# The last query tile of each batch takes the 64 rows that are left, in a fused attention and two-layer feed-forward kernel

## The chip, the cores and the metric

The kernel runs on one core of a Trainium2 chip. The metric is the device time of one execution in microseconds. The profile is of one execution; the runs that are compared are others.

## What is computed

The reference, cut to what matters (B = 8 batches, H = 8 heads, S = 576 rows, D = 64; all in float32):

```python
k_p = k.reshape(B, H, 72, 8, D).mean(axis=3)
v_p = v.reshape(B, H, 72, 8, D).mean(axis=3)
scores = scale * np.matmul(q, k_p.transpose(0, 1, 3, 2))
scores = scores - np.max(scores, axis=-1, keepdims=True)
attn = np.exp(scores)
attn = attn / (np.sum(attn, axis=-1, keepdims=True) + 1e-09)
attn_out = np.matmul(attn, v_p)

x = attn_out.transpose(0, 2, 1, 3).reshape(4608, 512)
h = x @ w_in
x = np.maximum(0.01 * h, h) @ w_out

rms = np.sqrt(np.mean(x * x, axis=-1, keepdims=True) + 1e-06)
xn = x / rms * rms_g
g = xn @ w_gate
out = (g * (1.0 / (1.0 + np.exp(-g))) * (xn @ w_val)) @ w_out2
```

## The kernel before

The program has three parts: attention, a first feed-forward layer (512 to 2048 to 512) and a second one (512 to 1536 to 512, with normalisation and gate). Attention is woven into the first layer: while the matmuls of one tile of 512 tokens of that layer run, the attention steps of later tokens are put between them. That weave fills the first 880 us; the second layer follows.

Attention goes batch by batch, 40 query tiles in all. The 576 query rows of a batch are five tiles of 128 (list `QT`, line 52), the fifth of which starts at row 448, so that its first 64 rows are rows of the fourth, taken again. The steps of a query tile (b, t) are:

- `load_q` (line 217): one DMA on SP's queue, 128 rows by 8 heads by 64 numbers, in pieces of 256 bytes.
- `step_t` (line 299): four TensorE transposes against the identity `ident`, tile `qt` (line 303), and a copy of the result to `qT` on ScalarE (line 308).
- `step_s` (line 313): four matmuls with the pooled keys, tiles `sc` (line 325), with `qT` as the stationary operand and 144 columns moving. The softmax runs with the query rows on the partitions: maximum, subtraction, exponential, sum, reciprocal, product (lines 331 to 340).
- `step_x` (line 347): the small copies `er` (line 363), four transposes `xt` (line 369), two transposes `xr` from 96 columns (line 374). From the result ScalarE writes the high halves of the weights, `at` (`split`, line 92) and `atr` (line 376), and VectorE their low halves (lines 95 and 378). Of the fifth tile the first 64 columns were left out here (`skip`).
- `step_av` (line 390): once both or all three tiles of a chunk (256 or 320 rows) are there, for each pair of heads three matmuls with `at` (line 395) and one with `atr` (line 400), tile `av`; its result is split into the tokens `xhl` of the first layer.

The names in the profile carry batch, chunk or tile: `at1_0` holds the weights of batch 1 (counted from 0), chunk 0; `xt1_1` the transposes of batch 1, tile 1; `xt2_4` those of the fifth tile of batch 2. In the profile's rows these numbers are left out.

Beside this, the first layer's weights come in during the first 130 us (`class Weights`): `load` (line 130, a DMA from SP), `begin` (a ScalarE and a VectorE instruction on the raw tile, lines 138 and 141), `end` (lines 149, 92 and 95). The last of them are loaded in halves, such as `raw_o14_256` and `raw_i15_256`, into three slots that they share with the loads of keys and values. In the first layer `h` (line 592) is x @ w_in for 512 tokens and 128 hidden columns, `ghl` its activation, `y` (line 628) the product with w_out; `y_store` (line 635) copies a finished `y` tile to `ye`, on ScalarE or VectorE by turns, and stores it.

The code gives each engine its instructions in program order, but for the first 880 us the framework's scheduler may put them in another order on each engine, by its own estimates of durations. That order is fixed when the program is built; on the chip each engine works through its list, and an instruction that waits holds up those behind it on the same engine.

Of the kernel before, what the change touches and what calls it, by code (L numbers as in the profile page):

```python
# [8 lines left out]
F32 = mybir.dt.float32  # L9
# [4 lines left out]
ALU = mybir.AluOpType  # L14
# [8 lines left out]
def pooled_attention_then_two_ffns(  # L23
# [13 lines left out]
    nc = tc.nc  # L37
    B, H, S, D = q.shape
    NT, DM = out.shape
    P = 128  # L40
    POOL = 8
    SP = S // POOL
    NP = H // 2
# [5 lines left out]
    W = 2 * P  # L49
    N = 512  # L50
    NJ = NT // N
    QT = [0, 128, 256, 384, S - P]
    RB = [0, 128, 256, 384, H * SP - P]
    CH = [(0, 256, (0, 1)), (256, S, (2, 3, 4))]
    CHMAX = 320
# [4 lines left out]
    REST = 2 * SP - P  # L60
    R1 = 2 * REST
    R3 = 3 * R1
# [6 lines left out]
    def bank(tag, bufs, name):  # L69
        return ps.tile([P, 512], F32, tag=tag, bufs=bufs, name=name)  # L70
# [7 lines left out]
    def scratch(b, name, early=False):  # L78

        return bank("att", 2, name) if b else bank("ya" if early else "yb", 2, name)  # L80

    ident = per.tile([P, P], F32, name="ident")
# [6 lines left out]
    def split(hi_eng, hi, lo_eng, lo, src):  # L89

        if hi_eng is nc.scalar:
            nc.scalar.activation(out=hi, in_=src, func=AF.Copy)  # L92
        else:
            hi_eng.tensor_copy(out=hi, in_=src)
        lo_eng.tensor_tensor(out=lo, in0=src, in1=hi.bitcast(F32), op=ALU.subtract)  # L95
# [8 lines left out]
    def rows(w, f):  # L104
        return w[f * P:(f + 1) * P, :]
# [62 lines left out]
    att = tc.tile_pool(name="att", bufs=1)  # L168
    ap = att.__enter__()
# [5 lines left out]
    for h, sign in ((0, -1), (1, 1)):  # L175
        nc.gpsimd.affine_select(
            out=mask_main[:, h:h + 1], in_=mask_main[:, h:h + 1], compare_op=ALU.is_ge, fill=0.0,
# [4 lines left out]
    for sign, base in ((1, 0), (-1, REST - 1)):  # L182
        nc.gpsimd.affine_select(
            out=group, in_=group, compare_op=ALU.is_ge, fill=0.0, base=base, channel_multiplier=sign,
# [4 lines left out]
        out=mask_rest[:, :, 1], in_=group.rearrange("p d q -> p q d"), axis=AX.X, op=ALU.add  # L189
# [27 lines left out]
    def load_q(b, t, tile_=None):  # L217
        x = ap.tile([P, 512], F32, tag="q", bufs=2, name=f"q{b}_{t}") if tile_ is None else tile_
        nc.sync.dma_start(
            out=x.rearrange("p (h d) -> p h d", h=H),  # L220
            in_=q[b, :, QT[t]:QT[t] + P, :].rearrange("h s d -> s h d"),
        )
        qraw[b, t] = x

# [74 lines left out]
    def step_t(b, t):  # L299
        pt = scratch(b, f"qt{b}_{t}", early=t < 2)  # L300
        x = qraw.pop((b, t))
        for c in range(NP):
            nc.tensor.transpose(pt[:, c * P:(c + 1) * P], x[:, c * P:(c + 1) * P], ident)  # L303
        if b == 0 and t % 3:
            y = per.tile([P, NP, P], F32, tag=f"w{23 + t % 3}", bufs=1, name=f"qT{b}_{t}")
        else:
            y = ap.tile([P, NP, P], F32, tag="qT", bufs=1, name=f"qT{b}_{t}")
        nc.scalar.copy(out=y.rearrange("p c n -> p (c n)"), in_=pt)
        qT[b, t] = y

    ex = {}
# [1 line left out]
    def step_s(b, t):  # L313
        y = qT.pop((b, t))
        if b == 0:
            e = per.tile([P, H, SP], F32, tag=f"w{20 + t % 4}", bufs=1, name=f"ex{b}_{t}")
        else:
            e = ap.tile([P, H, SP], F32, tag="ex", bufs=1, name=f"ex{b}_{t}")
        st = ap.tile([P, 3, H], F32, tag="st", bufs=2, name=f"st{b}_{t}")
        n = 2 * SP  # L320
        for half in range(2):
            pt = bank("att", 2, f"sc{b}_{t}_{half}")
            for i in range(2):
                p = 2 * half + i
                nc.tensor.matmul(  # L325
                    pt[:, i * n:(i + 1) * n], y[:, p, :], kblk[b % 2][:, p * n:(p + 1) * n],
                    start=True, stop=True,
                )
            s = pt[:, 0:2 * n].rearrange("p (h c) -> p h c", h=4)
            hs = slice(4 * half, 4 * half + 4)  # L330
            nc.vector.tensor_reduce(out=st[:, 0, hs], in_=s, axis=AX.X, op=ALU.max)
            nc.vector.tensor_tensor(
                out=e[:, hs, :], in0=s, in1=st[:, 0, hs].unsqueeze(2).to_broadcast([P, 4, SP]),
                op=ALU.subtract,
            )
        nc.scalar.activation(out=e, in_=e, func=AF.Exp, scale=ESCALE)
        nc.vector.tensor_reduce(out=st[:, 1, :], in_=e, axis=AX.X, op=ALU.add)
        nc.vector.tensor_scalar(out=st[:, 1, :], in0=st[:, 1, :], scalar1=1e-9, scalar2=None, op0=ALU.add)
        nc.vector.reciprocal(out=st[:, 2, :], in_=st[:, 1, :])
        nc.vector.tensor_tensor(  # L340
            out=e, in0=e, in1=st[:, 2, :].unsqueeze(2).to_broadcast([P, H, SP]), op=ALU.mult
        )
        ex[b, t] = e

# [2 lines left out]
    def step_x(b, t):  # L347
        ci = 0 if t < 2 else 1
        c0 = CH[ci][0]
        if (b, ci) not in at:  # L350
            at[b, ci] = (
                ap.tile([P, NP, 2, CHMAX], F32R, tag="at", bufs=1, name=f"at{b}_{ci}"),
                ap.tile([R3, 2, CHMAX], F32R, tag="atr", bufs=1, name=f"atr{b}_{ci}"),
            )
        a, ar = at[b, ci]
        e = ex.pop((b, t)).rearrange("p (c h) k -> p c (h k)", h=2)
        new = QT[t] if t < 4 else QT[3] + P
        skip = new - QT[t]
        n = P - skip
        cols = slice(new - c0, new - c0 + n)  # L360
        er = ap.tile([P, 2, 3, R1], F32, tag="er", bufs=1, name=f"er{b}_{t}")
        for g in range(2):
            (nc.scalar.copy if b < 2 else nc.vector.tensor_copy)(
                out=er[:, g].rearrange("p d (q k) -> p d q k", q=2),
                in_=e[:, 2 * g:2 * g + 2, P:].unsqueeze(1).to_broadcast([P, 3, 2, REST]),
            )
        pt = scratch(b, f"xt{b}_{t}")
        for c in range(NP):
            nc.tensor.transpose(pt[:, c * P:(c + 1) * P], e[:, c, 0:P], ident)  # L369
        src = pt.rearrange("p (c n) -> p c n", n=P)[:, :, skip:]  # L370
        split(nc.scalar, a[:, :, HI, cols], nc.vector, a[:, :, LO, cols], src)
        pt = scratch(b, f"xr{b}_{t}")
        for g in range(2):
            nc.tensor.transpose(pt[0:R3, g * P:(g + 1) * P], er[:, g].rearrange("p d k -> p (d k)"), ident)
        src = pt[0:R3, 0:2 * P].rearrange("p (g n) -> p g n", n=P)[:, :, skip:]
        nc.scalar.activation(out=ar[:, :, cols], in_=src, func=AF.Copy)
        z = slice(R1, 2 * R1)
        nc.vector.tensor_tensor(
            out=ar[z, :, cols], in0=src[z], in1=ar[z, :, cols].bitcast(F32), op=ALU.subtract
        )  # L380
# [171 lines left out]
    for n in range(2 * F1):  # L552
        key = ("io"[n % 2], n // 2)
        src = rows(w_out, n // 2) if n % 2 else cols(w_in, n // 2)
# [13 lines left out]
    for i in range(0, len(first), 2):  # L568
# [3 lines left out]
        t = per.tile([P, 2, 512], F32, tag=f"w{24 + i // 2}", bufs=1, name=f"first{i}")  # L572
# [689 lines left out]
```

## Time and profile before

| | us |
| --- | --- |
| median of 3 runs | 1808.96 (1805.79 to 1812.09) |
| the profiled execution | 1812.26 |
| its span | 1810.5 |
| PE busy (matmul) | 1758.0 (97%) |
| DVE, ACT, POOL busy | 891.1 (49%), 670.4 (37%), 551.2 (30%) |

PE is TensorE's matmuls, PEld its weight loads, DVE is VectorE, ACT ScalarE, POOL GpSimd and SP the engine that issues the DMAs. The span is the profiled execution from its first instruction to its last; its time is the 1810.5 us and 1.8 us around it. Matmuls are pipelined: the duration of a record is longer than the distance from one to the next, so costs on PE are read from the starts of groups. A number in square brackets at the end of a timeline row is the time that the engine stood idle before it, with the instruction or DMA that ended this.

### The profile page before, as it was taken

What the parts mean: (1) busy time and instruction counts of PE and PEld (TensorE: products, weight loads), DVE (VectorE), ACT (ScalarE), POOL (GpSimd) and SP (SyncE); (2) the same over time, 40 slices, a digit from 0 to 9 for tenths busy, and PEclk for the clock granted to TensorE, in tenths of its full rate; (3) what the DMA queues carried; (4) which work ended last, traced back from release to release, by engine and by line L of the source; (5) the groups of instructions that cost most, each with busy time, mean ns of one, the idle gap of its engine ahead of it and who ended that gap; (6) DMA issues with size and microseconds to landing.
All of it is one profiled execution on the core that took longest, in us unless ns stands there. A gap on an engine that the chain in (4) does not pass through costs nothing.

```text
span 1810.5 us, 23634 instructions
## 1 busy us (share of the span) xinstructions
PE 1758.0 (97%) x8596; PEld 1498.0 (83%) x8596; DVE 891.1 (49%) x1603; ACT 670.4 (37%) x1424; POOL 551.2 (30%) x681
## 2 busy tenths in 40 slices
PE   3899999999999999999999999999999999999999
PEld 2889887878888888888888888899788889978887
DVE  7974435454356555455344345345534444553331
ACT  5754333443344444344343332243232323322220
POOL 2653303334125142211110442154144204413320
PEclk6999999999999999999999999999999999999999
DMA  8833204447365555435451766687775668776562
GB/s 253 307 109 89 55 21 143 157 140 230 101 189 157 163 157 162 145 125 180 157 172 45 234 195 211 228 300 245 255 245 196 193 226 314 245 250 224 186 209 93
DMA packets 175555, 330.81 MB, mean 183 GB/s; under 512 B 54352, under 2 KB 90192, under 8 KB 174928
## 3 DMA queue, kind: packets, MB, share of 16 engines
q1 hardware_dynamic: 175440, 329.31, 56.1%
q8 instruction: 68, 1.11, 0.3%
q14 instruction: 47, 0.39, 0.1%
HBM read 277.87 MB, written 51.38 MB: 182 GB/s over the span
## 4 chain that ended last, share of the span: by engine, by line
PE 89%; DVE 5%; DMA 3%; issue 1%; ACT 1%; SPq 1%; POOL 1%; ACTq 0%; DVEq 0%; POOLq 0%
PE y L628 20%; PE h L592 20%; PE o L1089 16%; PE yg L1014 6%; PE yv L1014 6%; PE xv L1014 4%; PE xg L1014 4%; PE wg L1014 4%; PE wv L1014 4%; PE sc L325 2%; PE av L395 1%; PE xt L369 1%; DMA wo<-wo 1%; PE qt L303 1%; DMA y<-ye 1%
## 5 line engine op out<-in xcount | busy, mean ns | idle before, releaser
L592 PE MATMUL h<-xhl,w_i 128*128 128x512 f32 (+1 forms) x1824 | 438.2, 385 | 3.1 <-ACT xhl L92 1.3
L592 PEld LDWEIGHTS h<-xhl,w_i 128*128 128x128 f32 x1824 | 329.5, 191 | 68.3 <-DVE xhl L95 4.1
L1089 PE MATMUL o<-wo,u 128*128 128x512 f32 x1296 | 315.1, 390 | 3.5 <-DMA wo<-wo 3.4
L628 PE MATMUL y<-ghl,w_o 128*128 128x512 f32 (+1 forms) x1296 | 285.1, 365 | 1.4 <-DVE ghl L605 1.4
L1089 PEld LDWEIGHTS o<-wo,u 128*128 128x128 f32 x1296 | 242.0, 188 | 53.0 <-DMA wo<-wo 4.9
L628 PEld LDWEIGHTS y<-ghl,w_o 128*128 128x128 f32 x1296 | 218.9, 191 | 35.1 <-DVE ghl L605 1.8
L605 DVE TENSOR_TENSOR ghl<-g,ghl 128x512 fp32r<-128x512 f32 (+1 forms) x152 | 114.6, 754 | 241.5 <-ACT g L98 238.3
L98 ACT ACTIVATE ghl<-h 128x512 fp32r<-128x512 f32 (+1 forms) x152 | 87.0, 572 | 233.4 <-PE h L592 232.9
L628 PE MATMUL y<-ghl,wr 128*128 128x512 f32 x624 | 158.9, 395 | 0.0
L628 PEld LDWEIGHTS y<-ghl,wr 128*128 128x128 f32 x624 | 115.1, 188 | 22.4
L95 POOL TENSOR_TENSOR u<-e2g,u 128x512 fp32r<-128x512 f32 (+1 forms) x25 | 29.7, 1190 | 308.3 <-ACT u L92 308.3
L229 POOL TENSOR_TENSOR v<-v 128x256 f32<-128x256 f32 (+2 forms) x84 | 59.7, 713 | 107.6 <-DMA v<-in_v_dram 105.0
L98 ACT ACTIVATE g<-h 128x512 f32<-128x512 f32 (+1 forms) x152 | 86.8, 571 | 1.0 <-DVE ghl L605 1.0
L1014 PE MATMUL yg<-T,ag 128*128 128x512 f32 (+1 forms) x360 | 84.0, 368 | 0.0
L1014 PE MATMUL yv<-T,av 128*128 128x512 f32 (+1 forms) x360 | 83.8, 368 | 0.0
L1014 PE MATMUL xg<-xa,ag 128*128 128x512 f32 (+1 forms) x360 | 83.8, 367 | 0.0
L1014 PE MATMUL xv<-xa,av 128*128 128x512 f32 (+1 forms) x360 | 83.7, 367 | 0.0
L1014 PEld LDWEIGHTS yg<-T,ag 128*128 128x128 f32 x360 | 66.0, 188 | 10.0 <-DVE e1v L991 0.6
L1014 PEld LDWEIGHTS yv<-T,av 128*128 128x128 f32 x360 | 66.2, 188 | 9.5
L1014 PEld LDWEIGHTS xv<-xa,av 128*128 128x128 f32 x360 | 66.0, 188 | 9.6
L1014 PEld LDWEIGHTS xg<-xa,ag 128*128 128x128 f32 x360 | 66.1, 188 | 9.4
L735 POOL TENSOR_TENSOR parts_g<-raw_g,parts_g 128x256 fp32r<-128x256 f32 (+1 forms) x48 | 33.7, 727 | 102.7 <-ACT parts_g L731 102.7
(166 smaller groups left out, 2596.2 us busy)
## 6 DMA issues: line engine op xcount, KB each, us to landing
wo<-wo SPq DMA_DIRECT2D x120, 512.0 KB
av<-op_v SPq DMA_DIRECT2D x90, 512.0 KB
ag<-op_g SPq DMA_DIRECT2D x90, 512.0 KB
wr<-wo SPq DMA_DIRECT2D x52, 512.0 KB
y<-ye SPq DMA_DIRECT2D x36, 256.0 KB
op_g<-parts_g SPq DMA_DIRECT2D x36, 256.0 KB
op_v<-parts_v SPq DMA_DIRECT2D x36, 256.0 KB
out_dram<-oe SPq DMA_DIRECT2D x36, 256.0 KB
```

What stands on the lines that cost most here:

```text
L95: lo_eng.tensor_tensor(out=lo, in0=src, in1=hi.bitcast(F32), op=ALU.subtract)
L98: return nc.scalar.activation(out=out, in_=in_, func=AF.Prelu, scale=scale, alpha=alpha)
L229: nc.gpsimd.tensor_tensor(out=x[:, :n], in0=x[:, :n], in1=x[:, n:2 * n], op=ALU.add)
L303: nc.tensor.transpose(pt[:, c * P:(c + 1) * P], x[:, c * P:(c + 1) * P], ident)
L325: nc.tensor.matmul(pt[:, i * n:(i + 1) * n], y[:, p, :], kblk[b % 2][:, p * n:(p + 1) * n], start=True, stop=True,)
L369: nc.tensor.transpose(pt[:, c * P:(c + 1) * P], e[:, c, 0:P], ident)
L592: nc.tensor.matmul(pt, w[:, sp, c * P:(c + 1) * P], x[:, mp, c, :], start=c == 0 and i == 0, stop=c == n_k - 1 and i == 2,)
L605: nc.vector.tensor_tensor(out=t[:, LO, :], in0=g, in1=t[:, HI, :].bitcast(F32), op=ALU.subtract)
L628: nc.tensor.matmul(pt, w[:, sp, m * P:(m + 1) * P], g[:, mp, a - c0:a - c0 + n], start=ydone[j, a] == 1 and i == 0 and m % per_bank == 0, ...
L735: own(nc.gpsimd.tensor_tensor(out=d[:, :, LO, :], in0=x, in1=d[:, :, HI, :].bitcast(F32), op=ALU.subtract))
L1014: nc.tensor.matmul(pt, wt[:, a, c, sp, :], xt[:, mp, :], start=start and c == 0 and i == 0, stop=c == 1 and i == 2, skip_group_check=not s ...
L1089: nc.tensor.matmul(pt, u[:, sp, m * P:(m + 1) * P], w[:, mp, :], start=f == 0 and i == 0, stop=f == F2 - 1 and i == 2,)
```

## The change

The fifth tile starts at row 512 and has 64 rows, and `step_t`, `step_s` and `step_x` work on as many rows as the tile has. The four `qt`, four `xt` and two `xr` transposes of such a tile run with 64 columns of the identity in place of 128, over 64 rows; the columns of the stationary operand stay 128 (`xr`: 96). The four `sc` matmuls have 64 columns in the stationary operand and still 144 moving. The softmax works on 64 partitions with rows of the same length; the copy to `qT` has 256 in place of 512 numbers for each partition; the load of the queries is 128 KB in place of 256 KB. The results that are written to `at` and `atr` had 64 columns before and have 64 now. There are eight such tiles. The number of instructions of each engine is the same.

```diff
--- before.py
+++ after.py
@@ -49,7 +49,8 @@
     W = 2 * P
     N = 512
     NJ = NT // N
-    QT = [0, 128, 256, 384, S - P]
+    QT = [0, 128, 256, 384, 512]
+    QN = [P, P, P, P, S - 4 * P]
     RB = [0, 128, 256, 384, H * SP - P]
     CH = [(0, 256, (0, 1)), (256, S, (2, 3, 4))]
     CHMAX = 320
@@ -217,8 +218,8 @@
     def load_q(b, t, tile_=None):
         x = ap.tile([P, 512], F32, tag="q", bufs=2, name=f"q{b}_{t}") if tile_ is None else tile_
         nc.sync.dma_start(
-            out=x.rearrange("p (h d) -> p h d", h=H),
-            in_=q[b, :, QT[t]:QT[t] + P, :].rearrange("h s d -> s h d"),
+            out=x[0:QN[t], :].rearrange("p (h d) -> p h d", h=H),
+            in_=q[b, :, QT[t]:QT[t] + QN[t], :].rearrange("h s d -> s h d"),
         )
         qraw[b, t] = x
 
@@ -299,13 +300,15 @@
     def step_t(b, t):
         pt = scratch(b, f"qt{b}_{t}", early=t < 2)
         x = qraw.pop((b, t))
+        n = QN[t]
         for c in range(NP):
-            nc.tensor.transpose(pt[:, c * P:(c + 1) * P], x[:, c * P:(c + 1) * P], ident)
+            nc.tensor.transpose(pt[:, c * n:(c + 1) * n], x[0:n, c * P:(c + 1) * P], ident[0:n, 0:n])
         if b == 0 and t % 3:
             y = per.tile([P, NP, P], F32, tag=f"w{23 + t % 3}", bufs=1, name=f"qT{b}_{t}")
         else:
             y = ap.tile([P, NP, P], F32, tag="qT", bufs=1, name=f"qT{b}_{t}")
-        nc.scalar.copy(out=y.rearrange("p c n -> p (c n)"), in_=pt)
+        y = y.rearrange("p c n -> p (c n)")[:, 0:NP * n].rearrange("p (c n) -> p c n", n=n)
+        nc.scalar.copy(out=y, in_=pt[:, 0:NP * n].rearrange("p (c n) -> p c n", n=n))
         qT[b, t] = y
 
     ex = {}
@@ -317,9 +320,11 @@
         else:
             e = ap.tile([P, H, SP], F32, tag="ex", bufs=1, name=f"ex{b}_{t}")
         st = ap.tile([P, 3, H], F32, tag="st", bufs=2, name=f"st{b}_{t}")
+        m = QN[t]
+        e, st = e[0:m], st[0:m]
         n = 2 * SP
         for half in range(2):
-            pt = bank("att", 2, f"sc{b}_{t}_{half}")
+            pt = bank("att", 2, f"sc{b}_{t}_{half}")[0:m]
             for i in range(2):
                 p = 2 * half + i
                 nc.tensor.matmul(
@@ -330,7 +335,7 @@
             hs = slice(4 * half, 4 * half + 4)
             nc.vector.tensor_reduce(out=st[:, 0, hs], in_=s, axis=AX.X, op=ALU.max)
             nc.vector.tensor_tensor(
-                out=e[:, hs, :], in0=s, in1=st[:, 0, hs].unsqueeze(2).to_broadcast([P, 4, SP]),
+                out=e[:, hs, :], in0=s, in1=st[:, 0, hs].unsqueeze(2).to_broadcast([m, 4, SP]),
                 op=ALU.subtract,
             )
         nc.scalar.activation(out=e, in_=e, func=AF.Exp, scale=ESCALE)
@@ -338,7 +343,7 @@
         nc.vector.tensor_scalar(out=st[:, 1, :], in0=st[:, 1, :], scalar1=1e-9, scalar2=None, op0=ALU.add)
         nc.vector.reciprocal(out=st[:, 2, :], in_=st[:, 1, :])
         nc.vector.tensor_tensor(
-            out=e, in0=e, in1=st[:, 2, :].unsqueeze(2).to_broadcast([P, H, SP]), op=ALU.mult
+            out=e, in0=e, in1=st[:, 2, :].unsqueeze(2).to_broadcast([m, H, SP]), op=ALU.mult
         )
         ex[b, t] = e
 
@@ -354,25 +359,25 @@
             )
         a, ar = at[b, ci]
         e = ex.pop((b, t)).rearrange("p (c h) k -> p c (h k)", h=2)
-        new = QT[t] if t < 4 else QT[3] + P
-        skip = new - QT[t]
-        n = P - skip
-        cols = slice(new - c0, new - c0 + n)
-        er = ap.tile([P, 2, 3, R1], F32, tag="er", bufs=1, name=f"er{b}_{t}")
+        n = QN[t]
+        cols = slice(QT[t] - c0, QT[t] - c0 + n)
+        er = ap.tile([P, 2, 3, R1], F32, tag="er", bufs=1, name=f"er{b}_{t}")[0:n]
         for g in range(2):
             (nc.scalar.copy if b < 2 else nc.vector.tensor_copy)(
                 out=er[:, g].rearrange("p d (q k) -> p d q k", q=2),
-                in_=e[:, 2 * g:2 * g + 2, P:].unsqueeze(1).to_broadcast([P, 3, 2, REST]),
+                in_=e[:, 2 * g:2 * g + 2, P:].unsqueeze(1).to_broadcast([n, 3, 2, REST]),
             )
         pt = scratch(b, f"xt{b}_{t}")
         for c in range(NP):
-            nc.tensor.transpose(pt[:, c * P:(c + 1) * P], e[:, c, 0:P], ident)
-        src = pt.rearrange("p (c n) -> p c n", n=P)[:, :, skip:]
+            nc.tensor.transpose(pt[:, c * n:(c + 1) * n], e[:, c, 0:P], ident[0:n, 0:n])
+        src = pt[:, 0:NP * n].rearrange("p (c n) -> p c n", n=n)
         split(nc.scalar, a[:, :, HI, cols], nc.vector, a[:, :, LO, cols], src)
         pt = scratch(b, f"xr{b}_{t}")
         for g in range(2):
-            nc.tensor.transpose(pt[0:R3, g * P:(g + 1) * P], er[:, g].rearrange("p d k -> p (d k)"), ident)
-        src = pt[0:R3, 0:2 * P].rearrange("p (g n) -> p g n", n=P)[:, :, skip:]
+            nc.tensor.transpose(
+                pt[0:R3, g * n:(g + 1) * n], er[:, g].rearrange("p d k -> p (d k)"), ident[0:n, 0:n]
+            )
+        src = pt[0:R3, 0:2 * n].rearrange("p (g n) -> p g n", n=n)
         nc.scalar.activation(out=ar[:, :, cols], in_=src, func=AF.Copy)
         z = slice(R1, 2 * R1)
         nc.vector.tensor_tensor(
```

The scheduler takes the new sizes into its estimates, and so the lists of the engines change too, mostly within the first 130 us. Line numbers after the change are up to 5 higher. Two places follow; the last number of a name only counts tiles.

The first is DVE's list at about 120 us, where batch 1's first two query tiles become `at1_0` and `atr1_0` and the last halves of the weights (`raw_o14_256`, `raw_i15_0`, `raw_i15_256`, `raw_o15_0`) come in. Before:

```order
L141 TENSOR_SCALAR raw_o14_256_1423<-raw_o14_256_1423 128x256
L149 SCALAR_TENSOR_TENSOR raw_o14_256_1423<-raw_o14_256_1423 128x256
L95 TENSOR_TENSOR at1_0_1166<-xt1_1_1359,at1_0_1166 128x4x128
L378 TENSOR_TENSOR atr1_0_1167<-xr1_1_1366,atr1_0_1167 32x2x128
L95 TENSOR_TENSOR w_o14_1428<-raw_o14_256_1423,w_o14_1428 128x256
L272 TENSOR_TENSOR vb1_5_1351<-vm1_5_1349,vb1_5_1351 32x256
L141 TENSOR_SCALAR raw_i15_0_1431<-raw_i15_0_1431 128x256
L149 SCALAR_TENSOR_TENSOR raw_i15_0_1431<-raw_i15_0_1431 128x256
L141 TENSOR_SCALAR raw_i15_256_1438<-raw_i15_256_1438 128x256
L605 TENSOR_TENSOR ghl0_13_0_1385<-g0_13_0_1384,ghl0_13_0_1385 128x512
L141 TENSOR_SCALAR raw_o15_0_1526<-raw_o15_0_1526 128x256
L149 SCALAR_TENSOR_TENSOR raw_i15_256_1438<-raw_i15_256_1438 128x256
```

And with the change:

```order
L142 TENSOR_SCALAR raw_o14_256_1423<-raw_o14_256_1423 128x256
L150 SCALAR_TENSOR_TENSOR raw_o14_256_1423<-raw_o14_256_1423 128x256
L610 TENSOR_TENSOR ghl0_12_0_1265<-g0_12_0_1264,ghl0_12_0_1265 128x512
L96 TENSOR_TENSOR w_o14_1428<-raw_o14_256_1423,w_o14_1428 128x256
L142 TENSOR_SCALAR raw_i15_0_1431<-raw_i15_0_1431 128x256
L273 TENSOR_TENSOR vb1_5_1351<-vm1_5_1349,vb1_5_1351 32x256
L150 SCALAR_TENSOR_TENSOR raw_i15_0_1431<-raw_i15_0_1431 128x256
L142 TENSOR_SCALAR raw_i15_256_1438<-raw_i15_256_1438 128x256
L96 TENSOR_TENSOR at1_0_1166<-xt1_1_1359,at1_0_1166 128x4x128
L142 TENSOR_SCALAR raw_o15_0_1526<-raw_o15_0_1526 128x256
L150 SCALAR_TENSOR_TENSOR raw_i15_256_1438<-raw_i15_256_1438 128x256
L383 TENSOR_TENSOR atr1_0_1167<-xr1_1_1366,atr1_0_1167 32x2x128
```

`at1_0<-xt1_1` stood two rows behind the first row of `raw_o14_256`; now the row of `raw_i15_256` stands directly ahead of it. ACT's list has the same shift: its part of `at1_0` stood directly behind `raw_o14_256` and now stands behind `raw_i15_0`, and its part of `atr1_0` behind `raw_i15_256`. On PE the `av1_0_0` matmuls that wait for both stand, before and after, behind the same `y` matmuls with `ghl0_11`.

The second is ACT's list at about 280 us, at the end of batch 2's queries. Before:

```order
L308 COPY qT3_0_2859<-qt3_0_2854 128x512
L641 COPY ye1_0_1_2984<-y1_0_1_2229 128x512
L641 COPY ye1_0_3_2990<-y1_0_3_2231 128x512
L92 ACTIVATE at2_1_2638<-xt2_4_2878 128x4x64
L376 ACTIVATE atr2_1_2639<-xr2_4_2885 96x2x64
L92 ACTIVATE vb3_0_3045<-vm3_0_3043 128x128
```

And with the change:

```order
L311 COPY qT3_0_2859<-qt3_0_2854 128x512
L646 COPY ye1_0_1_2984<-y1_0_1_2229 128x512
L93 ACTIVATE at2_1_2638<-xt2_4_2878 128x4x64
L646 COPY ye1_0_3_2990<-y1_0_3_2231 128x512
L381 ACTIVATE atr2_1_2639<-xr2_4_2885 96x2x64
L93 ACTIVATE vb3_0_3045<-vm3_0_3043 128x128
```

ACT's part of `at2_1` now stands ahead of the copy `ye1_0_3` and not behind it, and that of `atr2_1` stands behind it still. The same exchange is made one batch later, with `at3_1` and `ye2_0_3`, at about 387 us.

## Rows read from the trace of the kernel before

**Rows 1.** Busy time by stretch: us of PE, PEld, DVE, ACT, POOL (instructions), PEclk, DMA share, GB/s

```profile
28.00:115.00 87.00, 71.75 (x461) 64.79 (x462) 85.98 (x161) 63.37 (x152) 48.38 (x57) 0.87 0.75 249
...
131.00:270.00 139.00, 138.89 (x829) 123.01 (x828) 60.46 (x126) 50.23 (x132) 40.07 (x76) 1.00 0.21 58
...
392.00:880.00 488.00, 484.89 (x2352) 404.63 (x2351) 252.74 (x536) 201.00 (x467) 140.55 (x228) 1.00 0.50 157
```

**Rows 2.** Waits of PE: in all, times, longest (us)

```profile
PE av L395 <- DVE at L95: 8.9, 4, 2.7
```

**Rows 3.** Tiles qt and xr, each form of weight load and matmul: ns least/median/most

```profile
L303 PEld LDWEIGHTS qt<-ident,q x140: 138/140/142, 76.8 to 828.7; 128*128 128x128 f32 x140
...
L374 PEld LDWEIGHTS xr<-ident,er x80: 123/127/203, 29.4 to 852.4; 128*96 128x96 f32 x80
```

**Rows 4.** Timeline of PE, 828 to 837 us: start, duration, work, count

```profile
828.46 0.60 PE L303 MATMUL qt<-ident,q 128*128 128x128 f32 x4
828.82 1.87 PE L628 MATMUL y<-ghl,wr 128*128 128x512 f32 x7
830.53 2.90 PE L592 MATMUL h<-xhl,w_i 128*128 128x512 f32 x12
833.26 0.60 PE L369 MATMUL xt<-ident,ex 128*128 128x128 f32 x4
833.70 0.38 PE L374 MATMUL xr<-ident,er 128*96 128x128 f32 x2
833.83 3.00 PE L628 MATMUL y<-ghl,wr 128*128 128x512 f32 x12
836.67 2.88 PE L592 MATMUL h<-xhl,w_i 128*128 128x512 f32 x12
```

**Rows 5.** Timeline of PE, 118 to 124 us, before the first query tiles of batch 1

```profile
118.43 1.71 PE L628 MATMUL y<-ghl,w_o 128*128 128x256 f32 x13
122.85 1.01 PE L395 MATMUL av<-at,vb 128*128 128x256 f32 x3 [2.71 <-DVE at L95]
123.66 0.41 PE L400 MATMUL av<-atr,vb 96*128 96x256 f32 x1
```

**Rows 6.** Timeline of ACT, the same place

```profile
120.46 0.44 ACT L98 ACTIVATE raw_o<-raw_o 128x256 f32<-128x256 f32 x1 [6.29 <-DMA raw_o<-in_moe_w_out_dram]
```

**Rows 7.** Timeline of DVE, 122 to 127 us

```profile
122.11 0.68 DVE L95 TENSOR_TENSOR at<-xt,at 128x512 fp32r<-128x512 f32 x1
122.82 0.42 DVE L378 TENSOR_TENSOR atr<-xr,atr 32x256 fp32r<-32x256 f32 x1
123.27 0.43 DVE L95 TENSOR_TENSOR w_o<-raw_o,w_o 128x256 fp32r<-128x256 f32 x1
...
126.17 0.70 DVE L141 TENSOR_SCALAR raw_i<-raw_i 128x256 int32<-128x256 uint32 x1 [1.11 <-DMA raw_i<-in_moe_w_in_dram]
```

**Rows 8.** Timeline of PE, the end of batch 2's queries

```profile
278.65 0.60 PE L369 MATMUL xt<-ident,ex 128*128 128x128 f32 x4
...
281.32 0.71 PE L395 MATMUL av<-at,vb 128*128 128x320 f32 x3 [1.85 <-DVE at L95]
281.87 0.31 PE L400 MATMUL av<-atr,vb 96*128 96x320 f32 x1
```

**Rows 9.** Timeline of ACT, the same place

```profile
279.93 0.58 ACT L641 COPY ye<-y 128x512 f32<-128x512 f32 x1 [1.58 <-DMA y<-ye]
280.41 0.39 ACT L92 ACTIVATE at<-xt 128x256 fp32r<-128x256 f32 x1
```

**Rows 10.** Timeline of PE, the end of batch 3's queries

```profile
388.23 0.71 PE L395 MATMUL av<-at,vb 128*128 128x320 f32 x3 [1.80 <-DVE at L95]
```

**Rows 11.** Busy time by stretch, around the three gaps

```profile
282.66:286.07 3.41, 3.41 (x9) 2.73 (x9) 1.51 (x6) 1.02 (x4) 1.44 (x4) 0.50 0.76 225
...
122.23:129.06 6.83, 6.21 (x24) 5.83 (x25) 5.40 (x13) 4.76 (x12) 1.89 (x5) 0.50 0.48 154
380.00:392.00 12.00, 10.12 (x52) 8.06 (x51) 7.25 (x17) 4.94 (x14) 1.89 (x3) 1.00 0.45 145
```

## Prediction

> **What bounds the kernel now.** I read the busy time by stretch first. From 28 to 115 us DVE is the bound, busy for 85.98 of 87 us; from 131 to 270 us it is PE, 138.89 of 139, and from 392 to 880 us PE again, 484.89 of 488 [rows 1]. So an instruction saved on PE counts one for one from 131 us to the end of the weave, and what PE loses before 131 us is not made up later. Next come the waits of PE: the only ones that the change touches are four waits of the `av` matmuls for the low halves that DVE writes, 8.9 us in all [rows 2]. The timelines show the three large ones: 2.71 us before 122.85 [rows 5], 1.85 before 281.32 [rows 8] and 1.80 before 388.23 [rows 10]. The stretches around them show the granted clock of PE: 0.50, its lower level of 1.2 GHz, from 122.23 to 129.06 and from 282.66 to 286.07, but 1.00 all through the third place [rows 11]. There are thus two kinds of term: transposes on PE, and waits that the new lists move.
>
> The sum is made against the profiled execution, 1812.26 us, which lies 3.3 us (0.18%) above the median of 1808.96; the difference that I find is applied to the median. About 0.3%, or 5.4 us, is what a measurement of this kernel can tell from no change.
>
> **Transposes.** What one costs is read from starts. Twelve `h` matmuls take from 830.53 to 833.26, 2.73 us or 0.2275 each. Four `qt` and seven `y` take 2.07 us (828.46 to 830.53); less 7 x 0.2275 that is 0.48 for the `qt`. Four `xt`, two `xr` and twelve `y` take 3.41 us (833.26 to 836.67); less 2.73 that is 0.68 for six [rows 4]. So ten transposes of a tile cost 1.16 us, 0.116 each. With half the moving columns I take half, 0.058 saved. On the path lie all ten of batches 1, 4, 5, 6 and 7. In batches 2 and 3 only the four `qt` do, since the `xt` and `xr` there run just ahead of a wait that is set by something else (below). Batch 0's lie in DVE's stretch and count nothing. That is 50 + 8 = 58 transposes, **-3.4 us**; all 80 would give -4.6, and none at all 0, since no row shows a transpose with 64 moving columns.
>
> Half is my choice and not certain, because the stationary operand keeps its 128 columns. The weight-load records are 140 ns for 128 columns and 127 for 96 [rows 3]: 13 ns for 32 columns, 52 for 128. That would fit under a transpose of 58 ns, so I take half; if it does not fit, the first rival holds. The Trainium skill speaks against the change here: "TensorE: Matmul & The Clock Gate", section "LDWEIGHTS (loading the stationary operand)", prices a weight load by its columns alone, whatever the rows, at P / 1.2 ns, 107 ns for 128 columns. By that the `qt` and `xt` would gain almost nothing and this term would be about -0.4. The difference of the two records here bears out the columns as the measure but half the price.
>
> **What else gets smaller.** The `sc` matmuls keep their 144 moving columns: nothing. The softmax runs on half the partitions with rows as long as before; DVE took 0.42 us for 32 partitions by 256 numbers and 0.43 for 128 by 256 [rows 7], so partitions don't count: nothing. The copy to `qT` falls from 512 to 256 numbers on ACT, which is no bound after 131 us: nothing, hidden under PE. The load is 128 KB shorter. No later tile waits for its queries, and in batch 0 the loads lie ahead of DVE's stretch; at that stretch's 249 GB/s [rows 1] it is 0.5 us at most, taken as 0.
>
> **The two waits that get shorter.** At 280 us ACT stood 1.58 us for the slot of a `ye` copy (held by a store) and began this copy at 279.93; its part of `at2_1` came behind it, at 280.41 [rows 9], and the first `av` 0.91 later, at 281.32 [rows 8]. The `xt` were ready at 278.65 + 0.60 = 279.25. With ACT's part ahead of the copy the first `av` can start at 279.25 + 0.91 = 280.16. `atr2_1` stays behind the copy and takes the place at 280.41; by the same 0.91 the fourth `av` is possible at 281.3 at the latest, where it ran at 281.87 [rows 8]. So between 0.6 and 1.2 us; I take 0.7, as the fourth `av` decides. The same at 387 us, where the wait was 1.80 [rows 10]: **-1.4 us** together (bounds -2.4 and -1.0). The half clock from 282.66 to 286.07 stands just behind the first of these waits. If it goes, 3.41 us of full work [rows 11] take 1.7 less. A wait of 1.80 at 387 us left the clock at 1.00 [rows 11], so one of 1.1 may well leave it too: **-1.7 us**, bounds -1.7 and 0.
>
> **The wait that grows.** At 120 us ACT and DVE stood for the load of `raw_o14_256`, which ACT began to work on at 120.46 [rows 6]. DVE's part of `at1_0` followed at 122.11 and the first `av` 0.74 later, at 122.85 [rows 5, 7]. The new list of DVE has that part directly behind the first row of `raw_i15_256`, which waited for its DMA until 126.17 and took 0.70 [rows 7]. PE has nothing to take in between: its list has `av1_0_0` at the same place. So `at1_0` comes at about 126.8 and the first `av` at 127.5, which is 4.7 us later. `atr1_0` stands three rows further back (0.68 + 0.3 + 0.4 by like rows), at about 128.2, and holds the fourth `av` until some 128.5, against 123.66: 4.8 later [rows 5]. Against that stands the clock. Before, nearly all of the stretch at 0.50 was busy (6.21 of 6.83 us, [rows 11]), which cost 3.1 us; now half of it or more would be idle. If the stretch ends at 129.06 again, about 1.3 us busy at half clock remain and 2.3 are given back; if the clock stays low as long after the restart as before, nothing is. I take the middle, 4.7 - 1.2 = **+3.5 us**, bounds +2.4 and +4.8. What is queued behind these instructions on DVE are the remaining weight halves and `xhl1`, needed only after the `av`.
>
> Sum: -3.4 - 1.4 - 1.7 + 3.5 = -3.0. The profiled execution would take 1809.3 us, the median 1806.0.
>
> **Rivals.**
> - *The weight load sets the pace of a transpose.* Then `qt` and `xt` stay at 0.116, and only the 96 columns of `xr` save a quarter, 0.03 each, ten of them on the path: -0.3 in place of -3.4, a total of +0.1, 1809.1. For it: the weight columns don't change. Against it: the 13 ns for 32 columns [rows 3].
> - *The wait at 120 us does not grow.* If the load of `raw_i15_256` lands before PE arrives, +3.5 becomes 0 or less: a total of -6.5, 1802.5. For it: DVE and ACT run other lists from the start, and a load that starts earlier lands earlier. Against it: it shares its three slots with the key and value loads, and it would have to be there 4 us earlier.
> - *Slower: the load lands later still.* The place is the same, and each microsecond that `raw_i15_256` lands after 126.17 is one lost by PE. With the full 4.8, no clock gained at 282.66 and transposes that save nothing the total is -0.3 - 1.4 + 4.8 = +3.1; a landing later by more than 2.3 us, at 128.5, makes it over +5.4. I price it at 3 us later, +6.1, 1815.1. For it: the queue is in order and raw slots are freed by work that the new lists also move. Against it: this needs three terms to fail at once, or a landing 8 us later if they hold.
> - *The change doesn't do what it says.* The lists show the smaller forms on every engine, so only what they are worth is open; no chance of its own beyond the first rival.
>
> **How the numbers follow.** Forecast 0.46, weight load 0.22, no growth 0.18, slower 0.14. Faster than 1803.5 needs the second rival, or the forecast with every bound at its good end: 0.22. Slower than 1814.4 is the third rival and a small tail of the first: 0.16. The rest, 0.62, is within 0.3%. The range reaches from the second rival with all 80 transposes and the lower bounds, -8, to between the forecast's bad end and the third rival, +5: 1801.0 to 1814.0.
>
> **What would show it.** Right: `qt` and `xt` of a fifth tile with starts some 0.06 us apart; `av` at about 280.2 and 387.1 less what PE has gained or lost until then, with `at` ahead of a `ye` copy on ACT; a clock of 1.00 behind it; a gap of about 7 us in front of `av1_0_0`, ended by DVE behind the DMA of `raw_i15_256`. Wrong: starts still 0.11 apart (first rival); a gap of 3 us or less there (second); a gap over 9 us (third). A difference after 880 us, where the lists are the same, would be none of this.

## The result and the profile after

The change makes the kernel slower: 1820.76 us median of 6 runs (1818.89 to 1823.67) against 1810.12 of 6 runs of the kernel before (1805.79 to 1812.09), a ratio of 1.0061 with a 95% interval of 1.0046 to 1.0076. The profiled execution took 1819.60 us, span 1817.6, where that of before took 1812.26. The forecast was 1806.0.

The busy time by stretch of the kernel after (columns as in [rows 1]):

```profile
28.00:115.00 87.00, 69.00 (x426) 61.45 (x425) 79.83 (x155) 60.12 (x143) 50.00 (x56) 0.92 0.73 244
...
392.00:880.00 488.00, 484.63 (x2333) 398.78 (x2334) 254.21 (x541) 200.68 (x471) 141.70 (x228) 1.00 0.50 158
```

Two things are to be seen. DVE, which bounded the stretch up to 115 us, is busy for 79.83 us in it, not for 85.98 [rows 1]: it waits now. And from 392 to 880 us PE is as full as before, yet it gets through 2333 matmuls there and not 2352: being busy, it does less.

The first point is explained by the waits of DVE from 40 to 112 us (in all, times, longest). Of the kernel before:

```profile
DVE ghl L605 <- ACT g L98: 0.2, 1, 0.2
```

And of the kernel after:

```profile
DVE st L336 <- PE sc L330: 4.1, 3, 3.1
DVE ghl L610 <- ACT g L99: 1.4, 1, 1.4
DVE vb L96 <- ACT vb L93: 0.5, 1, 0.5
DVE w_o L96 <- ACT w_o L93: 0.4, 1, 0.4
```

That is 6.4 us in place of 0.2. The longest, 3.12 us to 83.91, is for the scores of batch 1's first tile. In the list of before other work stood ahead of these maxima, and DVE came to them at 81.86 without a wait. The scores come later as well: PE began them at 80.84 before and begins them at 82.71 now. In the timeline of DVE, before:

```profile
81.86 0.46 DVE L331 TENSOR_REDUCE st<-sc 128x4 f32<-128x288 f32 x1
```

and after:

```profile
83.91 0.46 DVE L336 TENSOR_REDUCE st<-sc 128x4 f32<-128x288 f32 x1 [3.12 <-PE sc L330]
```

The place at 120 us, in the timeline of PE after:

```profile
123.34 1.71 PE L633 MATMUL y<-ghl,w_o 128*128 128x256 f32 x13
129.69 1.01 PE L400 MATMUL av<-at,vb 128*128 128x256 f32 x3 [4.63 <-DVE at L96]
```

of DVE:

```profile
128.74 0.29 DVE L142 TENSOR_SCALAR raw_i<-raw_i 128x256 int32<-128x256 uint32 x1 [1.39 <-POOL w_i L96]
128.95 0.68 DVE L96 TENSOR_TENSOR at<-xt,at 128x512 fp32r<-128x512 f32 x1
```

and of ACT, on the same half of a weight:

```profile
128.81 0.45 ACT L99 ACTIVATE raw_i<-raw_i 128x256 f32<-128x256 f32 x1 [1.00 <-DMA raw_i<-in_moe_w_in_dram]
```

The wait that was forecast is there: `at1_0` comes directly behind the row of `raw_i15_256`, and the gap of PE is 4.63 us where it was 2.71 [rows 5]. It is not the 7.4 that was forecast, since PE came to it late: at 129.69 - 4.63 = 125.06, against 120.14 before. But the load came late too. SP issued it at 125.86, against 123.24 before, and DVE could work on it at 128.74, against 126.17 [rows 7]. So the first `av` starts 6.84 us later than before, not the 4.7 of the forecast. PE's own lateness is not what sets this start, as PE stands until `at1_0` is there: without the wait 125.06 would be 2.2 us later than 122.85.

The end of batch 2's queries, PE after:

```profile
287.34 0.71 PE L400 MATMUL av<-at,vb 128*128 128x320 f32 x3 [0.82 <-DVE at L96]
288.19 0.42 PE L405 MATMUL av<-atr,vb 96*128 96x320 f32 x1
```

and ACT:

```profile
286.45 0.38 ACT L93 ACTIVATE at<-xt 128x256 fp32r<-128x256 f32 x1 [0.89 <-PE xt L372]
287.06 0.58 ACT L646 COPY ye<-y 128x512 f32<-128x512 f32 x1 [0.24 <-DMA y<-ye]
```

Here the forecast holds: ACT's part of `at2_1` no longer stands behind the copy that waits for a slot, and the gap is 0.82 in place of 1.85 [rows 8]; one batch later it is 0.82 in place of 1.80 [rows 10].

The second point, that PE does less in the same time, shows in the fifth tile of batch 4, in the timeline of PE after:

```profile
528.11 0.61 PE L597 MATMUL h<-xhl,w_i 128*128 128x512 f32 x2
528.65 0.70 PE L330 MATMUL sc<-kblk,qT 128*64 128x144 f32 x4
529.28 0.98 PE L597 MATMUL h<-xhl,w_i 128*128 128x512 f32 x3
530.19 0.70 PE L330 MATMUL sc<-kblk,qT 128*64 128x144 f32 x4
530.83 1.89 PE L597 MATMUL h<-xhl,w_i 128*128 128x512 f32 x7
532.55 2.88 PE L633 MATMUL y<-ghl,wr 128*128 128x512 f32 x12
...
538.49 0.84 PE L633 MATMUL y<-ghl,wr 128*128 128x512 f32 x3
539.26 0.46 PE L372 MATMUL xt<-ident,ex 64*128 64x64 f32 x4
539.66 0.96 PE L633 MATMUL y<-ghl,wr 128*128 128x512 f32 x3
540.55 0.31 PE L377 MATMUL xr<-ident,er 64*96 64x64 f32 x2
540.79 1.66 PE L633 MATMUL y<-ghl,wr 128*128 128x512 f32 x6
542.28 2.90 PE L597 MATMUL h<-xhl,w_i 128*128 128x512 f32 x12
```

From 528.11 to 532.55 there are twelve `h` and two groups of `sc` (two matmuls of two passes each): 4.44 - 12 x 0.2275 = 1.71 us, or 0.85 for a group. The same tile before:

```profile
523.61 0.40 PE L592 MATMUL h<-xhl,w_i 128*128 128x512 f32 x1
523.84 0.66 PE L325 MATMUL sc<-kblk,qT 128*128 128x144 f32 x4
524.24 1.19 PE L592 MATMUL h<-xhl,w_i 128*128 128x512 f32 x4
525.26 0.65 PE L325 MATMUL sc<-kblk,qT 128*128 128x144 f32 x4
525.66 1.89 PE L592 MATMUL h<-xhl,w_i 128*128 128x512 f32 x7
527.39 2.44 PE L628 MATMUL y<-ghl,wr 128*128 128x512 f32 x10
```

By the same reading these two groups cost 3.78 - 2.73 = 1.05 us, 0.53 each. From 538.49 to 542.28 four `xt` and two `xr` cost 3.79 - 2.73 = 1.06 us, where they cost 0.68 [rows 4], although they have half the columns. No wait is marked in any of these rows.

### The profile page after: what moved, and what is told of

The parts are those of the page before. It is cut to its first block, busy times and chain, and to the rows that moved or that the text cites. A ratio compares the mean times of both kernels' runs of the same rounds, so it can differ in the third digit from the quotient of the medians.

```text
span 1817.6 us, 23635 instructions
## 1 busy us (share of the span) xinstructions
PE 1764.8 (97%) x8596; PEld 1495.9 (82%) x8596; DVE 889.3 (49%) x1603; ACT 669.2 (37%) x1424; POOL 554.3 (30%) x681
## 4 chain that ended last, share of the span: by engine, by line
PE 90%; DMA 3%; DVE 2%; issue 2%; POOL 2%; SPq 1%; ACT 1%; ACTq 0%; POOLq 0%; DVEq 0%
PE y L633 21%; PE h L597 20%; PE o L1094 15%; PE yg L1019 6%; PE yv L1019 6%; PE xg L1019 4%; PE xv L1019 4%; PE wg L1019 4%; PE wv L1019 4%; PE sc L330 2%; PE av L400 1%; POOL w_i L96 1%; PE qt L305 1%; PE xt L372 1%; DMA wo<-wo 1%
```

## The experiments

All kernels but one were timed in five rounds against the kernel before; each ratio is followed by its 95% interval. The short tiles were switched by batch. With a batch's tile left as it was, the lists of the places that it doesn't touch are those of before, so the parts can be taken one at a time:

```diff
+    def short(b, t):
+        return t == 4 and b >= 4
+    def size(b, t):
+        return 64 if short(b, t) else P
...
-            nc.tensor.transpose(pt[:, c * P:(c + 1) * P], x[:, c * P:(c + 1) * P], ident)
+            nc.tensor.transpose(pt[:, c * n:(c + 1) * n], x[0:n, c * P:(c + 1) * P], ident[0:n, 0:n])
```

**Batches 4 to 7 alone** (`b >= 4`).

> Only the last tiles of batches 4 to 7 have 64 rows; the lists up to 500 us are those of before. Theory (each group of 64-wide matmuls or transposes that is entered from 128-wide work and left again costs PE some 0.34 us, beside transposes that do halve): slower by 2 to 3.5 us, as the trace of the change falls back by 3.0 us from 393 to 880 us; groups of four sc cost 1.33 us in place of 1.00. Rival of the forecast (only the halving): faster by 2.3 us. Rival weight load: no difference.

Measured 1813.72 us against 1809.83, ratio 1.0026 (1.0013 to 1.0038): slower by 3.9. The groups cost what they cost in the full change: four `sc` in a row 1.33 us, four `qt` 0.59. The lists of DVE and POOL are those of before throughout, so this is the price of the 64-wide work and of one exchange on ACT (a `ye` copy ahead of a part of `xhl7`, after which PE waits 0.77 us at 798 us). The halving alone and "no difference" both fall.

**Batch 0 alone** (`b == 0`).

> Only the last tile of batch 0 has 64 rows. Theory (the early loss comes from the new lists, which this one tile brings about, and not from the tile's own work): slower by 5 to 8 us, all of it before 131 us, with DVE idle in front of the maxima of sc1_0 at about 81 us and a gap of PE before av1_0_0. Rival (the early loss comes from the 64-wide groups of batch 0 and batch 1 themselves): under 1.5 us.

Measured 1819.83 against 1809.83, ratio 1.0060 (1.0044 to 1.0076): slower by 10.0, somewhat above what was expected. One tile of forty brings nearly all of the loss of the change. PE comes to the gap before `av1_0_0` at 124.51 us and leaves it at 129.36.

**Batches 2 and 3 alone** (`b in (2, 3)`).

> Only the last tiles of batches 2 and 3 have 64 rows; the early lists are those of before. Theory: the two exchanges on ACT and the clock behind the first give 3.1 us, the 64-wide groups of two tiles take back some 1: faster by 1.5 to 3 us. Rival (the exchanges give nothing where the rest is as before): slower by about 1.

Measured 1810.24 against 1809.83, ratio 1.0000 (0.9990 to 1.0011). The gaps are 0.82 us each, as in the change, but the time does not fall: the interval leaves a gain of 1.8 us at most. The groups of the two tiles take back 0.9 us of the 2.0 that the gaps give (`qt` with `kt` 0.77 in place of 0.67, four `sc` 1.33 in place of 1.00, twice each), and at 399 us PE stands 1.30 us for `ghl` in this trace, where it does not wait in that of before. The clock is part of it. In the run of batches 4 to 7 alone, where these lists are those of before, the gap was 1.77 us and the clock stayed at 1.00 behind it:

```profile
274.00:290.00 16.00, 14.23 (x75) 11.83 (x74) 7.80 (x21) 7.62 (x22) 6.80 (x15) 1.00 0.59 175
```

So the half clock from 282.66 to 286.07 [rows 11] does not come with this gap each time. Of the eight traces with a gap of 1.74 to 2.01 us at this place, four have a stretch at half clock behind it (0.91 in the mean from 270 to 290 us) and four have 1.00; the five with a gap of 0.77 to 0.92 all have 1.00. What the shorter gap wins in clock is thus some share of 1.7 us, and these runs do not tell how much. The stretch from 122.23 to 129.06 [rows 11] comes and goes in the same way: the run of batches 4 to 7 has 1.00 from 116 to 131 us, the kernel before 0.77.

**96 rows in place of 64**, in batches 1 to 6 (`return 96 if short(b, t) else P`, with 32 rows taken twice).

> The last tiles of batches 1 to 6 take 96 rows (32 of them twice) and their transposes 96 columns; all lists but one place on PE are those of before. Theory (the price of a group is one of 64-wide work only, as the 96-wide xr and av of before show none): ten transposes a tile save 0.03 each, faster by 1 to 2 us, and sc groups stay at 1.00. Rival (any shape under 128 pays it): slower by 2 to 4 us, with sc groups at 1.33.

Measured 1808.79 against 1809.83, ratio 0.9996 (0.9986 to 1.0006): no difference by itself, but the groups decide between the theories. The fifth tile of batch 4:

```profile
522.16 0.40 PE L605 MATMUL h<-xhl,w_i 128*128 128x512 f32 x1
522.40 0.65 PE L335 MATMUL sc<-kblk,qT 128*96 128x144 f32 x4
522.79 1.19 PE L605 MATMUL h<-xhl,w_i 128*128 128x512 f32 x4
523.82 0.65 PE L335 MATMUL sc<-kblk,qT 128*96 128x144 f32 x4
524.22 1.89 PE L605 MATMUL h<-xhl,w_i 128*128 128x512 f32 x7
525.95 2.44 PE L641 MATMUL y<-ghl,wr 128*128 128x512 f32 x10
...
531.90 1.30 PE L641 MATMUL y<-ghl,wr 128*128 128x512 f32 x5
533.03 0.49 PE L382 MATMUL xt<-ident,ex 96*128 96x96 f32 x4
533.37 0.33 PE L387 MATMUL xr<-ident,er 96*96 96x96 f32 x2
533.48 1.86 PE L641 MATMUL y<-ghl,wr 128*128 128x512 f32 x7
535.18 2.89 PE L605 MATMUL h<-xhl,w_i 128*128 128x512 f32 x12
```

From 522.16 to 525.95 the two `sc` groups cost 3.79 - 2.73 = 1.06 us, 0.53 each as before; four `xt` and two `xr` cost 3.28 - 2.73 = 0.55 (one group here, as in [rows 4]), less than the 0.68 of 128 columns. With 96 rows nothing is paid for the group and the columns save what they should. The price is one of 64, not of every shape under 128.

**Groups of 64-wide matmuls, counted.** Tiles of 128 rows again; the `sc` matmuls of the fifth tile are cut into two halves:

```diff
-                nc.tensor.matmul(
-                    pt[:, i * n:(i + 1) * n], y[:, p, :], kblk[b % 2][:, p * n:(p + 1) * n],
-                    start=True, stop=True,
-                )
+                for z in ((0, 64), (64, P)) if t == 4 and (b in (4, 5) or b > 5 and i) else ((0, P),):
+                    nc.tensor.matmul(
+                        pt[z[0]:z[1], i * n:(i + 1) * n], y[:, p, z[0]:z[1]],
+                        kblk[b % 2][:, p * n:(p + 1) * n], start=True, stop=True,
+                    )
```

> Last tiles of 128 rows; their sc matmuls are cut into two of 64 stationary columns, in batch 4 and 5 all of them (batch 5: eight in a row), in batch 6 and 7 every second one (128, 64, 64, 128, 64, 64). Theory (a price of 0.34 us for each group, not for each matmul): the eight cost 2.0 + 0.34 = 2.33 us, the mixed ones 1.5 + 2 x 0.34 = 2.18 us. Rival (each 64-wide matmul costs a quarter more): 2.67 and 1.83 us.

Batch 5 (eight in a row), then batch 6 (128, 64, 64, 128, 64, 64), in the timeline of PE:

```profile
626.06 2.20 PE L629 MATMUL y<-ghl,wr 128*128 128x512 f32 x9
628.19 1.20 PE L326 MATMUL sc<-kblk,qT 128*64 128x144 f32 x16
629.32 0.96 PE L629 MATMUL y<-ghl,wr 128*128 128x512 f32 x3
630.12 2.21 PE L593 MATMUL h<-xhl,w_i 128*128 128x512 f32 x9
...
732.32 2.21 PE L629 MATMUL y<-ghl,wr 128*128 128x512 f32 x9
734.37 1.65 PE L326 MATMUL sc<-kblk,qT 128*128 128x144 f32 x12
735.95 0.96 PE L629 MATMUL y<-ghl,wr 128*128 128x512 f32 x3
736.75 2.44 PE L593 MATMUL h<-xhl,w_i 128*128 128x512 f32 x10
```

The eight cost 4.06 - 2.73 = 1.33 us and the mixed ones 4.43 - 2.73 = 1.70. Both figures of both theories miss, for a reason that neither had: the two halves of a pair run at the same time (their records start 0.007 us apart in the trace, and the pairs some 0.12), so that eight matmuls of 64 columns take as long as four of 128 (1.00). With that the price of a group stands: 1.00 + 0.33 for one group, 2 x 0.25 + 2 x (0.25 + 0.35) = 1.70 for two. A price for each matmul doesn't fit: the mixed case has half as many 64-wide matmuls and pays twice as much.

**Batch 0's short tile with the load of before.** The queries are loaded as 128 rows, and the tile works on the last 64 of them; all 64-wide work stays.

```diff
-            out=x[0:size(b, t), :].rearrange("p (h d) -> p h d", h=H),
-            in_=q[b, :, (S - size(b, t) if t == 4 else QT[t]):(S if t == 4 else QT[t] + P), :].rearrange("h s d -> s h d"),
+            out=x.rearrange("p (h d) -> p h d", h=H),
+            in_=q[b, :, QT[t]:QT[t] + P, :].rearrange("h s d -> s h d"),
...
-            nc.tensor.transpose(pt[:, c * n:(c + 1) * n], x[0:n, c * P:(c + 1) * P], ident[0:n, 0:n])
+            nc.tensor.transpose(pt[:, c * n:(c + 1) * n], x[P - n:P, c * P:(c + 1) * P], ident[P - n:P, P - n:P])
```

> As the run with batch 0's short tile alone, but its queries are loaded as before (128 rows) and the tile works on the last 64 of them; with that the lists are those of before up to about 75 us, and the part of at1_0 stands directly behind raw_o14_256 again. Theory (the early loss is that of the lists: DVE's wait at 81 us and the later place of at1_0): within 2.5 us of before, with a gap of 2 to 3 us before av1_0_0. Rival (the 64-wide groups of batch 0 cost it): slower by 8 us or more, as with the short load.

Measured 1811.99 against 1808.22, ratio 1.0019 (1.0009 to 1.0029): slower by 3.8, where the short load made it 10.0. That is above the 2.5 of the theory (though 2.5 lies in the interval, 1.6 to 5.2) and well under the 8 of the rival. DVE waits from 40 to 112 us for 1.5 us in this kernel, all of it for scores.

**Batch 0 with 96 rows**, short load included.

> The last tile of batch 0 alone, with 96 rows: DVE's list changes in 124 places from the start on, but at1_0 stays directly behind raw_o14_256. Theory (the place of at1_0 and what follows it make most of the early loss): within 4 us of before, gap before av1_0_0 of 2 to 3 us. Rival (any list other than that of before loses the early 6 to 10 us): slower by 6 us or more.

Measured 1817.44 against 1808.22, ratio 1.0043 (1.0031 to 1.0055). Here the theory fell and the rival held: there is no 64-wide work in this kernel, `at1_0` stands where it stood, the gap before `av1_0_0` is 2.17 us, and still most of the loss is there. DVE's waits from 40 to 112 us:

```profile
DVE st L341 <- PE sc L335: 3.6, 2, 2.8
DVE xhl L101 <- ACT xhl L98: 0.8, 2, 0.7
```

So new early lists lose most of it even where `at1_0` keeps its place. The time at which PE comes to the gap before `av1_0_0` (start less idle time) puts the early part of the kernels side by side, with DVE's waits from above; the last column is the two others of PE added up:

| kernel | PE at the gap, us | DVE waits 40 to 112, us | the gap, us | first `av`, us |
| --- | --- | --- | --- | --- |
| before | 120.14 | 0.2 | 2.71 | 122.85 |
| batches 4 to 7 alone (early lists of before) | 119.37 | 0.6 | 2.56 | 121.93 |
| batch 0, 64 rows, load of before | 121.40 | 1.5 | 2.91 | 124.31 |
| batch 0, 96 rows | 124.17 | 4.4 | 2.17 | 126.34 |
| batch 0, 64 rows | 124.51 | 5.2 | 4.85 | 129.36 |
| the change | 125.06 | 6.4 | 4.63 | 129.69 |
| before, load cut in two (next run) | 119.17 | 1.5 | 2.35 | 121.52 |

PE is late by about as much as DVE waits, but for the last row. The 64-wide work is not what sets it (third and fourth row). Nor is it the landing of the smaller load: from 14 to 131 us no engine waits for a query load in the traces of before, of the change and of the three kernels with batch 0 alone. What the traces leave is the lists.

What is lost by the first `av` is another matter, since PE stands there in each of these kernels until a load has landed. With 96 rows it is `raw_o14_256`, as before, which SP issued at 118.44, against 115.23. With batch 0 alone at 64 rows and in the change `at1_0` has the later place, and the first `av` comes another 3.0 to 3.4 us later. By the medians that place is worth less (10.0 us lost against 9.2), so how the loss divides between late loads and the later place is not settled.

**The same work in another early list.** The kernel before, with the load of batch 0's last tile cut in two:

```diff
+        for z in ((0, 64), (64, P)) if (b, t) == (0, 4) else ((0, P),):
+            nc.sync.dma_start(
+                out=x[z[0]:z[1], :].rearrange("p (h d) -> p h d", h=H),
+                in_=q[b, :, QT[t] + z[0]:QT[t] + z[1], :].rearrange("h s d -> s h d"),
+            )
```

> The kernel before, with the queries of batch 0's last tile loaded by two DMAs of 64 rows in place of one of 128: the same bytes and the same work on every engine, but DVE's list differs from that of before in 99 places from the start on, and at1_0 stays where it was. Theory (another early list is what costs, whatever brings it about): slower by 3 us or more, with DVE idle between 48 and 110 us where before it is not. Rival (the 64-row or 96-row tile of batch 0 itself costs): no difference.

Measured 1812.73 against 1809.27, ratio 1.0019 (1.0009 to 1.0028): slower by 3.5, as the theory said, but not for its reason. DVE does wait, for 1.5 us, but PE comes to the gap at 119.17 us, as early as with the lists of before. So another early list need not lose where this one was expected to, and where these 3.5 us are lost stays open: single traces of equal lists differ by about as much.

**All batches but 0** (`b >= 1`).

> All last tiles but batch 0's have 64 rows. Theory (the lists that batch 0's tile brings about, and the 64-wide groups, are two separate losses): slower than before by 2 to 5 us, and with batch 0 alone (10.0) this makes up the 10.6 of the change within the intervals. Rival (the groups cost little and late losses came from the early ones): no difference.

Measured 1811.88 against 1809.27, ratio 1.0017 (1.0008 to 1.0027): slower by 2.6. With batch 0's 10.0 that makes 12.6, against 10.6 for the whole change, whose interval reaches from 8.3 to 13.8.

**A version that beats both.** First the slot alone: the fourth copy `ye` of token tiles 1 and 2 takes a slot of `ghl`, which is free there, and ACT no longer waits for a store.

```diff
-                t = per.tile([P, N], F32, tag="tg", bufs=3, name=f"ye{j}_{a}_{m}")
+                if m == 3 and j in (1, 2):
+                    t = per.tile([P, 2, N], F32R, tag="ghl", bufs=3, name=f"ye{j}_{a}_{m}").bitcast(F32)[:, 0, :]
+                else:
+                    t = per.tile([P, N], F32, tag="tg", bufs=3, name=f"ye{j}_{a}_{m}")
```

> The kernel before, with the fourth copy of y of token tiles 1 and 2 in a slot of ghl, which is free there, in place of the third slot of tg, which waits for a store. Theory (the wait of ACT for this slot sets the two gaps of PE at 280 and 387 us): the gaps fall from 1.8 to 0.8 us each, faster by 1.5 to 2.5 us, up to 4 if the clock stays up behind them. Rival (the gaps come from the weight halves being late anyway): no difference.

Measured 1808.19 against 1808.22, ratio 0.9992 (0.9982 to 1.0002): not told from no difference, although both gaps shrink to 0.77 us. The first:

```profile
277.47 0.71 PE L395 MATMUL av<-at,vb 128*128 128x320 f32 x3 [0.77 <-DVE at L95]
```

Then the slot together with tiles of 96 rows in batches 1 to 6:

> The same slot for ye, and last tiles of 96 rows in batches 1 to 6. Theory: both gains add up, faster by 2.5 to 4.5 us than before. Rival (the 96-row tiles give nothing beyond noise): as the run with the slot alone.

Measured 1806.64 against 1808.22, ratio 0.9987 (0.9978 to 0.9995): faster than before by 0.9 to 4.0 us, just clear of no difference, and so faster than the change too. The two parts together are resolved, neither is alone.

## Why the prediction was wrong

The forecast was -3.0 us and the result +10.6. Two steps failed: the price of the 64-wide shapes, and the early lists, which were read at one place with the landing times of before.

- **"With half the moving columns I take half, 0.058 saved", and -3.4 in all.** The half is right: behind the first transpose of a group the starts are 0.06 us apart (539.38, 539.44 and 539.50 for `xt` of batch 4), and the first rival (the weight load sets the pace) is out. What was missing is a price for the shape itself. Each group of 64-wide transposes or matmuls between 128-wide ones costs 0.32 to 0.35 us beyond its matmuls, so that even the halved transposes cost more than the whole ones: four `qt` 0.59 in place of 0.45, two `xr` 0.46 in place of 0.23, and two or four `sc`, of which the forecast said "nothing", 0.85 and 1.33 in place of 0.53 and 1.00. From 260 to 880 us the trace has 20 such groups whose cost can be read, and together they cost 4.1 us more than before. The term was at least +4.1, not -3.4. Batches 4 to 7 alone and all but batch 0, both slower, show that this loss stands by itself. The Trainium skill has the rule that speaks against the change, not on the page that was weighed but in "TensorEngine Tiling (Array Packing)", section "Key Properties": a change of the tiling mode drains the engine. The price of 0.32 to 0.35 us for going in and out fits that, but no row names the mode, so the drain as its cause is not shown. The same section's statement that tiles work in parallel agrees with the eight halves that took as long as four whole ones.
- **"Batch 0's lie in DVE's stretch and count nothing", and the early lists read at one place.** The forecast looked at the list of DVE around 120 us and at nothing ahead of it. There the new lists make DVE, the bound of that stretch, wait 6.4 us, PE comes to the place at 120 us late by 4.9 us, and the loads on which it waits there are issued late as well. Batch 0's tile alone costs 10.0 us. The kernel with 96 rows shows that the shape is not the cause, the one with the old load that most of it goes when the lists up to about 75 us are the old ones again. That the smaller load sets the scheduler on other lists is told by the lists themselves; that the lists, and not something else about the smaller load, cost the time is argued from what the traces leave, as no kernel has the one without the other.
- **"The wait that grows", +3.5.** Its mechanism is there, behind `raw_i15_256`, but the term was too small: the first `av` came 6.84 us later, not 4.7. The forecast had the load land when it did before; it was issued 2.62 us later. The gap itself grew by 1.9 us only, since PE arrived late too. Nor was the 1.2 us of clock given back: the half clock lasts 6.83 us as before, now from 128.89 to 135.72, and PE is busy for 6.04 of them, where it was for 6.21 [rows 11].
- **"The two waits that get shorter", -1.4.** Right in the trace: 0.82 us in place of 1.85 and 1.80, and the fourth `av` at 288.19, 0.85 behind the first, as the copy of `ye` ahead of `atr2_1` made likely. In time, batches 2 and 3 alone gave nothing that could be told from no change; their 64-wide groups and a new wait at 399 us take back about as much.
- **The clock, -1.7.** The kernel after has 1.00 there, as forecast. But four of the eight traces with the longer gap have 1.00 too, so the whole 1.7 was too much: a stretch at half clock in one profiled execution was taken for a property of the kernel.
- **"ACT copy, softmax, load: nothing."** The softmax on 64 partitions did cost the same, 0.86 us for 64 by 576 against 0.88 for 128 by 576. No engine waits for the smaller load, but as an input to the scheduler it was, as far as the runs tell, the dearest part of the change.

The slower rival came out in sign and, in part, in mechanism: `raw_i15_256` could be worked on 2.6 us after 126.17, and transposes saved nothing, which the rival asked for together. What it lacked is the price of the 64-wide groups.

In the pair of traces the terms close: +6.8 at the first `av`, +4.1 for the groups, -2.0 for the two gaps and -1.7 for the clock make 7.2, and the spans differ by 7.1. The medians differ by 10.6 (8.3 to 13.8); what they have beyond the traces is not placed.

## What to carry to other kernels

Before narrowing an operand of a matmul or transpose, look whether the narrow shape stands between full ones: here each such group of 64 cost 0.32 to 0.35 us, more than the halved columns of four transposes gave back, while 96 cost nothing. Where a scheduler orders the instructions by its estimates, a smaller transfer can change the order of a whole stretch; read the lists of the engine that bounds each stretch from the first difference on, not only at the place where one expects it. Where an engine waits for a load, ask what sets the load's issue, as it moves with the lists. And before a stretch at half clock is booked as a cost, see whether it is there in a second execution.

## What was not expected of the hardware

- A group of 64-wide work (64 rows in the stationary operand, or 64 columns) costs TensorE 0.32 to 0.35 us beyond its matmuls here, for two matmuls as for eight; with 96 the same groups cost nothing extra (0.53 us for two `sc`, as with 128).
- Two matmuls with 64 stationary columns that write to the two halves of the partitions run at the same time, with starts 0.007 us apart: eight took 1.33 us with the price of their group, 1.00 without it, as four of 128 columns do.
